# Lead and first block of an attention and two-layer MLP kernel emitted from one list, with five raw buffers, selected diagonals and sums per head pair

## Chip, cores and metric

One core of a Trainium2 chip runs the whole program. The metric is the device time of one execution in microseconds. The kernel before takes 912.47 us (median of three runs, 911.75 to 913.42).

## What is computed

A linear attention with decay over 4 batches, 8 heads, 768 steps and head size 48, then two MLP layers over the 3072 tokens of width 384 with hidden width 2048:

```python
for t in range(S):
    cur = np.einsum('bhd,bhe->bhde', u[None] * kt, vt)
    y[:, :, t] = np.einsum('bhd,bhde->bhe', rt, state + cur)
    state = w[None, :, :, None] * state + np.einsum('bhd,bhe->bhde', kt, vt)
x = y as (3072, 384)
r = np.maximum(x @ w_in, 0.0);  x = (r * r) @ w_out
h = x @ moe2_w_in;              out = (h - np.tanh(h)) @ moe2_w_out
```

## The kernel before

**Tiles.** The sequence is cut into 24 chunks of 128 steps, numbered 0 to 23: 0 to 3 are the first chunks of the four batches, 4 to 7 the second, and so on. Four chunks are one block of 512 tokens, so there are six blocks. Each MLP layer has 16 units of 128 hidden features. One unit of one block is a first product `gemm1` (tile `h`, nine matmuls of 512 columns), an activation, and a second product `gemm2` (three tiles `acc`, nine matmuls). Matmuls keep precision by parts: a weight is split in a high and a low part, so is the activation (`ghi`, `glo`), and three of the four products are summed.

**Weights** come as 64-bit numbers in raw tiles (`load_w`) and are converted by `conv0` (ScalarE, ACT), `conv1` (two instructions of VectorE, DVE), `conv2` (ACT, the high part) and `conv3` (DVE, the low part `w`). Layer 1's 16 weight tiles are converted while block 0 runs, one unit after the other. Layer 1 has four raw buffers; layer 2 takes two more from another pool.

**Lead.** The first four chunks need no state. `lead_a` multiplies r by k (`pr`) and applies the decays; `lead_p` forms the sums of u r k per step and head by matmul (tile `pk`, one matmul of 128 columns of weights per head pair) and transposes k; `lead_pa` copies both out on ACT and writes the diagonals of the score tile `am`; `lead_b` makes scores, `lead_m` masks them, `lead_c` makes the output y and the state, `lead_e` splits y into the tile `xt` that `gemm1` reads.

**Chunks from 4 on.** `load` fetches a chunk, `att_a` applies the decays (DVE), `att_k` the decay of the keys in natural order (GpSimd, POOL), `att_b` the scores `sc`, `att_v` the state update `pv`, `att_m` masks the scores into `ra`, whose diagonal holds u r k; `att_c` makes `y`, `att_e` splits it, `pack` moves 16 rows a head by six DMAs into place in `xt`. For chunks 4 to 7 the diagonal's sums come from matmuls (`att_diag`: 16 matmuls with one column, one per half chunk, head pair and head), are copied out by ACT, and are spread on the diagonal by one product with an identity on POOL (`att_d`) and eight activations on ACT (`att_da`). From chunk 8 on POOL and a DVE reduction make the sums, and POOL writes both halves of the diagonal.

**Order.** Instructions are issued per engine in the order in which the program emits them, and so are the DMAs of the queue SP. The lead is written out as a loop over four chunks at lines 870 to 915; block 0 is a loop over units in which `STEPS0` sets the units at which chunks 4 to 7 take their steps, and `gemm2`'s `glo` products are put off by one unit (`low_of`). Two lists are kept ahead: `front` issues `gemm1` and the activation two units early, `nat_q` holds POOL's work. Blocks 1 to 4 follow a fixed table (`visit`).

Of the kernel before, what the change touches and what calls it, by code (L numbers as in the profile page):

```python
# [25 lines left out]
def decay_attention_moe_moe_kernel(  # L26
# [10 lines left out]
    nc = tc.nc  # L37
# [11 lines left out]
    STEPS0 = ((1, 2, 3), (4, 5, 6), (8, 9, 10), (12, 13, 14))  # L49
    FILL = (0, 0, 4, 4)  # L50
# [179 lines left out]
    table = []  # L230

    def table_c():
        nc.vector.tensor_tensor(w96, pw[:, 0, :, 64:65], pw[:, 0, :, 32:33], op=ALU.mult)
        kh = gp.tile([GP, NP, L], F32, tag="g", name="kh")
# [3 lines left out]
        table.append(kh)  # L238

    def table_d():  # L240
        kh = table.pop()
        pt = bank(2, "pt")
        for p in range(NP):
            for a in range(2):
                q = slice(64 * a, 64 * a + D)
                nc.tensor.matmul(
                    pt[half(a), p * D:(p + 1) * D], lhsT=kh[q, p, :], rhs=ident[q, q], start=True, stop=True,
                )
        nc.scalar.activation(out=kt_tab, in_=pt[:, 0:GPS], func=AF.Copy)
# [39 lines left out]
    def att_s(i):  # L289
        bt_t[i] = a2.tile([128, 2, NP], F32, tag="bt", name="bt")  # L290
        nc.vector.tensor_reduce(
            out=bt_t[i].rearrange("p c P -> p (c P)"), in_=rn_t[i].rearrange("p (x d) -> p x d", d=D),
            axis=mybir.AxisListType.X, op=ALU.add,
        )
# [3 lines left out]

    def att_d(i, a):
        q = half(a)  # L300
        nc.gpsimd.tensor_tensor(
            ra_t[i][q, a],
            ident[q, q][:, None, None, :].to_broadcast([64, NP, 2, L]),
            bt_t[i][q].rearrange("p c (P o) -> p P c o", o=1).to_broadcast([64, NP, 2, L]),
            op=ALU.mult,
        )

    def att_da(i, a):
        q = half(a)
        for c in range(2):  # L310
            for p in range(NP):
                nc.scalar.activation(
                    out=ra_t[i][q, a, p, c, :], in_=ident[q, q], func=AF.Copy, scale=bt_t[i][q, c, p:p + 1]
                )

    def att_a(i):
        def sub(t):
            return t.rearrange("p P (c t) -> p P c t", c=2)

        def tab(t, n):  # L320
            return t[:, :, None, :].to_broadcast([n, NP, 2, L])

        r, k = rk_t[i][:, 0], rk_t[i][:, 1]
        if i < 2 * TPB:
            pr_t[i] = a2.tile([GP, NP, C], F32, tag="pr", name="pr")
            nc.vector.tensor_tensor(pr_t[i], r, k, op=ALU.mult)
            nc.vector.tensor_tensor(sub(r), sub(r), tab(tr[:, :, 32:96], GP), op=ALU.mult)
            for a in range(2):
                q = slice(64 * a, 64 * a + D)
                nc.sync.dma_start(out=ra_t[i][q, a].rearrange("p P c t -> p (P c t)"), in_=r[q].rearrange("p P t -> p (P t)"))  # L330
        else:
            for a in range(2):
                q = slice(64 * a, 64 * a + D)
                nc.vector.tensor_tensor(ra_t[i][q, a], sub(r[q]), tab(tr[q][:, :, 32:96], D), op=ALU.mult)
        nc.vector.tensor_tensor(sub(k), sub(k), tab(tr[:, :, 95:31:-1], GP), op=ALU.mult)
# [3 lines left out]
    def nat_push(i):  # L339
        if i < NTAU:  # L340
            G = nc.gpsimd
            if i < 2 * TPB:
                nat_q.append(lambda: att_k(i, G))
                return
# [27 lines left out]
    def att_diag(i, pb):  # L372
        bt = pb[:, 2 * GPS:2 * GPS + 2 * NP].rearrange("p (c P) -> p c P", c=2)
        for c in range(2):
            for p in range(NP):
                for a in range(2):
                    q = slice(64 * a, 64 * a + D)
                    nc.tensor.matmul(
                        bt[half(a), c, p:p + 1], lhsT=pr_t[i][q, p, c * L:(c + 1) * L],
                        rhs=ucol[q, p, a:a + 1], start=True, stop=True,  # L380
                    )
        bt_t[i] = a2.tile([128, 2, NP], F32, tag="bt", name="bt")
        nc.scalar.activation(out=bt_t[i], in_=bt, func=AF.Copy)
        att_d(i, 0)
        att_da(i, 1)

    def att_v(i):
        pb = pbank(i, 1, "pv")
# [10 lines left out]
        if i < 2 * TPB:  # L399
            att_diag(i, pb)  # L400
# [54 lines left out]
    def att_e(i):  # L455
# [24 lines left out]
    def lead_a(i):  # L480
        V = nc.vector
        r, k = rk_t[i][:, 0], rk_t[i][:, 1]
        V.tensor_tensor(pr_t[i], r, k, op=ALU.mult)
        if i:
            V.tensor_tensor(k, k, tk, op=ALU.mult)
            V.tensor_tensor(r, r, tr, op=ALU.mult)
            return
        up, down = pw[:, 0, :, 0:64], pw[:, 1, :, 64:0:-1]
        V.tensor_tensor(k[:, :, 0:64], k[:, :, 0:64], pw[:, 0, :, 63::-1], op=ALU.mult)
        V.tensor_tensor(k[:, :, 64:C], k[:, :, 64:C], pw[:, 1, :, 1:65], op=ALU.mult)  # L490
        V.tensor_tensor(r[:, :, 0:64], r[:, :, 0:64], down, op=ALU.mult)
        V.tensor_tensor(r[:, :, 64:C], r[:, :, 64:C], up, op=ALU.mult)
# [4 lines left out]
    def lead_p(i):  # L497
        pk = bank(1, "pk")
# [5 lines left out]
        for p in range(NP):  # L504
            nc.tensor.transpose(pk[:, p * GP:(p + 1) * GP], rk_t[i][:, 1, p, :], ident[0:GP, 0:GP])
        pk_t[i] = pk

    def lead_pa(i):
        pk = pk_t.pop(i)
        diag[i] = a2.tile([128, H], F32, tag="bt", name="bt0")  # L510
        nc.scalar.activation(out=diag[i], in_=pk[:, NP * GP:NP * GP + H], func=AF.Copy)
        nc.scalar.activation(
            out=kv_t[i][0], in_=pk[:, 0:NP * GP].rearrange("p (P x) -> p P x", x=GP), func=AF.Copy
        )
# [571 lines left out]
```

## Time and profile before

| | |
|---|---|
| median of three runs | 912.47 us |
| the profiled execution | 910.81 us |
| its span in the trace | 909.1 us |
| PE busy | 888.6 us, 98% |
| ACT busy | 640.3 us, 70% |
| DVE busy | 621.5 us, 68% |
| POOL busy | 219.5 us, 24% |
| mean granted clock of TensorE | 0.997 |
| one raw weight tile, by SP | 768 KB |
| one chunk: `rkt`, `kn`, two `vs` | 448, 192, 2 x 96 KB |
| one copy of `ra` | 96 KB, two a chunk |

Engines are called PE (TensorE, matmuls; PEld is its weight load), DVE, ACT, POOL, and SP for the DMA queue. An idle time in brackets is the time for which the engine waited just before the row, and behind the arrow stands what ended it. A matmul of full-precision numbers runs as two passes, so the trace shows twice as many as the program's rows.

### The profile page before, as it was taken

To read this page: it belongs to the slowest core of one execution; us is meant where nothing else is said; L and a number is where in the kernel's file an instruction comes from. 1 tells how busy PE (TensorE), PEld (TensorE's weight loads), DVE (VectorE), ACT (ScalarE), POOL (GpSimd) and SP (SyncE) were. 2 spreads that over 40 slices of the span, in tenths; PEclk is the share of its full clock that TensorE was granted. 3 is DMA by queue.
4 is the path that set the end of the run, shared out by engine and by line. 5 is a ranking of instruction groups with operands and counts; after the bars stand their busy time and mean duration, and the time that the engine had idled before them with its cause. 6 is when DMAs were issued, how large, how long until landed. Compare 5 with 4: busy or idle time off the path is not lost.

```text
span 909.1 us, 15201 instructions
## 1 busy us (share of the span) xinstructions
PE 888.6 (98%) x5852; PEld 732.2 (81%) x5852; DVE 621.5 (68%) x1003; ACT 640.3 (70%) x1163; POOL 219.5 (24%) x204
## 2 busy tenths in 40 slices
PE   9799999999999999999999999999999999999997
PEld 7677788888888888888888777888888888888885
DVE  7788942531432252221377899999999999999996
ACT  5777754455444544454688888988988988988985
POOL 5211424554464456353101021001001010010000
PEclk9999999999999999999999999999999999999999
DMA  9766321312222131200763200200200200200000
GB/s 257 204 196 201 113 87 51 100 54 67 71 69 69 52 102 52 83 9 8 271 218 137 70 1 0 70 1 1 70 0 1 70 1 1 69 1 1 35 0 36
DMA packets 31177, 65.98 MB, mean 73 GB/s; under 512 B 5264, under 2 KB 16912, under 8 KB 31104
## 3 DMA queue, kind: packets, MB, share of 16 engines
q1 hardware_dynamic: 30976, 64.78, 22.9%
q8 instruction: 46, 0.75, 0.3%
q14 instruction: 27, 0.22, 0.1%
q10 hardware_dynamic: 128, 0.23, 0.1%
HBM read 52.79 MB, written 9.44 MB: 68 GB/s over the span
## 4 chain that ended last, share of the span: by engine, by line
PE 85%; DMA 4%; DVE 4%; ACT 4%; issue 2%; SPq 1%; POOL 0%; DVEq 0%; POOLq 0%; ACTq 0%
PE h L628 39%; PE o L786 20%; PE acc L676 20%; DMA raw<-in_w_dram 2%; PE sc L367 2%; PE y L447 2%; PE pv L394 2%; DMA first_v<-in_nat_dram 1%; DMA ra<-rkt 1%; DVE hy L732 1%; ACT raw L85 0%; SPq L474 0%; DVE raw L94 0%; ACT th L733 0%; DVE hy L751 0%
## 5 line engine op out<-in xcount | busy, mean ns | idle before, releaser
L628 PE MATMUL h<-xt,w 128*128 128x512 f32 x864 | 212.4, 390 | 1.6 <-ACT w L102 0.9
L628 PE MATMUL h<-xs,w 128*128 128x512 f32 x864 | 211.4, 389 | 0.0
L628 PEld LDWEIGHTS h<-xt,w 128*128 128x128 f32 x864 | 162.5, 188 | 36.4 <-ACT w L102 1.3
L628 PEld LDWEIGHTS h<-xs,w 128*128 128x128 f32 x864 | 162.2, 188 | 34.0
L642 ACT ACTIVATE g<-h 128x512 f32<-128x512 f32 x96 | 57.2, 596 | 150.4 <-PE h L628 150.3
L676 PE MATMUL acc<-ghi,w 128*128 128x512 f32 x576 | 152.8, 397 | 6.1 <-ACT ghi L645 6.1
L786 PE MATMUL o<-ghi,w 128*128 128x512 f32 x576 | 148.8, 390 | 0.3 <-ACT ghi L757 0.3
L676 PEld LDWEIGHTS acc<-ghi,w 128*128 128x128 f32 x576 | 106.6, 189 | 29.9 <-ACT ghi L645 7.5
L786 PEld LDWEIGHTS o<-ghi,w 128*128 128x128 f32 x576 | 107.6, 188 | 24.0 <-ACT ob L797 1.3
L466 DVE TENSOR_TENSOR ys<-y,ys 112x128 fp32r<-112x128 f32 x20 | 5.8, 292 | 172.0 <-ACT xt L464 172.0
L648 POOL TENSOR_TENSOR glo<-g,ghi 128x512 fp32r<-128x512 f32 x64 | 82.1, 1283 | 169.2 <-PE acc L676 98.6
L709 POOL TENSOR_TENSOR xs<-x2f,xs 128x512 fp32r<-128x512 f32 x18 | 24.4, 1355 | 313.5 <-DVE xs L708 313.5
L733 ACT ACTIVATE th<-h 128x512 f32<-128x512 f32 x96 | 57.5, 599 | 41.9 <-DVE hy L732 41.9
L786 PE MATMUL o<-glo,w 128*128 128x512 f32 x288 | 84.2, 394 | 2.0 <-DVE glo L763 1.9
L676 PE MATMUL acc<-glo,w 128*128 128x512 f32 x288 | 83.2, 390 | 0.9 <-DVE glo L657 0.9
L746 DVE SCALAR_TENSOR_TENSOR hy<-q,hy 128x512 f32<-128x512 f32 x96 | 78.2, 815 | 0.1
L732 DVE SCALAR_TENSOR_TENSOR hy<-h,y 128x512 f32<-128x512 f32 x96 | 66.0, 687 | 13.4 <-ACT y L730 13.3
L751 DVE COPY_PREDICATED hy<-mask,th 128x512 f32<-128x512 uint8 x96 | 70.8, 737 | 0.0
L736 DVE TENSOR_TENSOR th<-h,th 128x512 f32<-128x512 f32 x96 | 66.2, 689 | 5.9 <-ACT th L733 0.7
L734 ACT ACTIVATE q<-y,ba 128x512 f32<-128x512 f32 x96 | 68.7, 715 | 0.0
L737 ACT ACTIVATE q<-y,bb 128x512 f32<-128x512 f32 x96 | 68.5, 713 | 0.0
L740 ACT ACTIVATE mask<-y,bm 128x512 uint8<-128x512 f32 x96 | 68.3, 711 | 0.0
(113 smaller groups left out, 1191.7 us busy)
## 6 DMA issues: line engine op xcount, KB each, us to landing
raw<-in_w_dram SPq DMA_DIRECT2D x32, 768.0 KB, 5.1
rkt<-in_rk_dram SPq DMA_DIRECT2D x20, 448.0 KB, 4.1
x2d<-x2s SPq DMA_DIRECT2D x18, 256.0 KB, 2.3
x2f<-x2d SPq DMA_DIRECT2D x18, 256.0 KB, 3.5
out_dram<-ob SPq DMA_DIRECT2D x18, 256.0 KB, 2.2
kn<-in_nat_dram SPq DMA_DIRECT2D x20, 192.0 KB, 4.8
vs<-in_nat_dram SPq DMA_DIRECT2D x40, 96.0 KB, 4.2
rnt<-in_nat_dram SPq DMA_DIRECT2D x16, 192.0 KB, 4.5
```

Of the source, the lines that this page charges most:

```text
L628: nc.tensor.matmul(h, lhsT=w_in(layer, f, part, kk), rhs=x[:, xpart, kk, :], start=(n == 0), stop=(n == 3 * KK - 1),)
L648: nc.gpsimd.tensor_tensor(lo, g, hi.bitcast(F32), op=ALU.subtract)
L676: nc.tensor.matmul(acc[j][m], lhsT=w_out(1, e, part, m * 128, (m + 1) * 128), rhs=g, start=(f == 0 and n < KK), stop=(last and g is lo),)
L732: nc.vector.scalar_tensor_tensor(out=hy, in0=h, scalar=PK, in1=y, op0=ALU.mult, op1=ALU.mult)
L733: nc.scalar.activation(out=th, in_=h, func=AF.Tanh)
L734: nc.scalar.activation(out=q1, in_=y, func=AF.Square, bias=p2["ba"], scale=1.0)
L736: nc.vector.tensor_tensor(th, h, th, op=ALU.subtract)
L737: nc.scalar.activation(out=q2, in_=y, func=AF.Square, bias=p2["bb"], scale=1.0)
L740: nc.scalar.activation(out=mask, in_=y, func=AF.Sign, bias=p2["bm"], scale=1.0)
L746: nc.vector.scalar_tensor_tensor(out=hy, in0=q2, scalar=PD, in1=hy, op0=ALU.add, op1=ALU.mult)
L751: nc.vector.copy_predicated(hy, mask, th)
L786: nc.tensor.matmul(acc[j][m], lhsT=w_out(2, f, part, m * 128, (m + 1) * 128), rhs=g, start=(f == 0 and n == 0), stop=(f == NF - 1 and n == 2),
```

## The change

Seven things are changed.

- Lead and block 0 are one list, `first_order`, of 419 pieces such as `h.3` (the `gemm1` of unit 3) or `c1a.5` (the first instruction of `conv1` of weight tile 5). A function per name emits the piece; the steps of the old functions are split so that each can stand by itself. The list also holds the DMAs. It covers block 0, the first two `gemm1` of block 1 and the first steps of chunks 8 and 9. `STEPS0`, `low_of` and the loop of the lead are gone.
- Five raw buffers in one pool serve both layers.
- The diagonal of `ra` is written by an affine selection on POOL that reads the sums with a broadcast and keeps them where row and column agree; for all chunks from 4 on, both halves. `att_da` on ACT is gone.
- The sums of chunks 0 to 7 are made per head pair: eight matmuls with 112 x 64 weights and two columns in place of 16 matmuls with one column (chunks 4 to 7), or of four with 112 x 128 weights (chunks 0 to 3). ACT copies them out by four small activations for chunks 4 to 7.
- The decay of the keys in natural order runs on DVE for chunks 4 to 7.
- `rn` and `pr` share one tile; `att_s` writes its eight sums in another order.
- The second head quartet's diagonals in the lead are indexed by a general formula, with the same result.

```diff
     def load_w(layer, f):
-        pool, n = (cv, 4) if layer == 1 or f % 5 < 3 else (p2["pool"], 2)
-        raw = pool.tile([128, 2 * DM, 2], U32, tag="raw", name="raw", bufs=n)
+        raw = cv.tile([128, 2 * DM, 2], U32, tag="raw", name="raw", bufs=5)
...
+    def diagonal(out, values):
+        m, n, t = out.shape
+        nc.gpsimd.affine_select(
+            out=out, in_=values[:, :, None].to_broadcast([m, n, t]), compare_op=ALU.is_equal, fill=0.0, base=0,
+            pattern=[[0, n], [1, t]], channel_multiplier=-1,
+        )
+
     def att_d(i, a):
         q = half(a)
-        nc.gpsimd.tensor_tensor(
-            ra_t[i][q, a],
-            ident[q, q][:, None, None, :].to_broadcast([64, NP, 2, L]),
-            bt_t[i][q].rearrange("p c (P o) -> p P c o", o=1).to_broadcast([64, NP, 2, L]),
-            op=ALU.mult,
-        )
-
-    def att_da(i, a):
...
+        diagonal(ra_t[i][q, a].rearrange("p P c t -> p (P c) t"), bt_t[i][q])
...
-    def att_diag(i, pb):
-        bt = pb[:, 2 * GPS:2 * GPS + 2 * NP].rearrange("p (c P) -> p c P", c=2)
-        for c in range(2):
-            for p in range(NP):
-                for a in range(2):
-                    q = slice(64 * a, 64 * a + D)
-                    nc.tensor.matmul(
-                        bt[half(a), c, p:p + 1], lhsT=pr_t[i][q, p, c * L:(c + 1) * L],
-                        rhs=ucol[q, p, a:a + 1], start=True, stop=True,
-                    )
...
+    def att_sums(i):
+        bt = sum_t[i] = pb_t[i][:, 2 * GPS:2 * GPS + 2 * NP].rearrange("p (P a) -> p P a", a=2)
+        for p in range(NP):
+            for c in range(2):
+                nc.tensor.matmul(
+                    bt[64 * c:64 * c + 64, p, :], lhsT=pr_t[i][:, p, c * L:(c + 1) * L], rhs=ucol[:, p, :],
+                    start=True, stop=True,
+                )
...
+        for a in range(2):
+            for c in range(2):
+                nc.scalar.activation(out=bt_t[i][half(a), c::2], in_=bt[64 * c:64 * c + 64, :, a], func=AF.Copy)
...
+    def lead_sums(i):
+        pk = pk_t[i] = bank(1, "pk")
         for p in range(NP):
-            nc.tensor.matmul(
-                pk[:, NP * GP + 2 * p:NP * GP + 2 * p + 2], lhsT=pr_t[i][:, p, :], rhs=ucol[:, p, :],
-                start=True, stop=True,
-            )
+            for c in range(2):
+                nc.tensor.matmul(
+                    pk[64 * c:64 * c + 64, NP * GP + 2 * p:NP * GP + 2 * p + 2],
+                    lhsT=pr_t[i][:, p, c * L:(c + 1) * L], rhs=ucol[:, p, :], start=True, stop=True,
+                )
...
+    first_order = """
+        pr.0 pb.0 rk.2 rk.1 tk.0 v.1 k.0 r.0 tp.0 pr.2 pr.1 v.0 rk.3 L.4 kn.0 lb.0 lb.1 k.1 lbt.0 dg.0 pb.1
...
+        "nk": lambda i: att_k(i, V if i < 2 * TPB else G),
...
+        for item in first_order.split():
+            what, which = item.split(".")
+            make[what](int(which))
+        del acc[0]
+
+        nf = NF + 2
         for n, (layer, j, f) in enumerate(units):
+            if n < NF:
+                continue
```

How the order moves shows at three places. The first is PE at the attention of chunk 5. Before, its scores (`sc`), state update (`pv`) and sums (`pv` from `wu` and `pr`) stand together ahead of the `gemm2` of unit 2:

```order
L628 MATMUL h<-xt,w_3_662 128x512 x9
L367 MATMUL sc<-ra_103,rkt 64x64 x16
L394 MATMUL pv<-vs_99,kn_101 64x48 x16
L378 MATMUL pv<-wu,pr 64x1 x16
L676 MATMUL acc_671<-ghi,w_2_629 128x512
```

Now they are three visits with other products between them:

```order
L382 MATMUL sc<-ra_103,rkt 64x64 x16
L739 MATMUL acc_664<-glo,w_0_557 128x512
L739 MATMUL acc_665<-glo,w_0_557 128x512
L739 MATMUL acc_666<-glo,w_0_557 128x512
L414 MATMUL pv<-vs_99,kn_101 64x48 x16
L691 MATMUL h<-xt,w_4_727 128x512 x9
L393 MATMUL pv<-wu,pr 64x2 x8
L691 MATMUL h<-xt,w_5_740 128x512 x9
```

The low products of unit 0 and the `gemm1` of units 4 and 5 have moved in between, and the sums are half as many matmuls. The second place is DVE around the first converted weight tiles (the `raw` rows are the two instructions of `conv1`, the `w` rows are `conv3`, the rows to `xt` the low parts of the lead's y). Before:

```order
L108 TENSOR_TENSOR w_0_448<-raw,w_0_448 128x768
L419 TENSOR_TENSOR dec<-st,pw 112x192
L610 TENSOR_TENSOR xt<-y,xt 128x3x128
L93 TENSOR_SCALAR raw<-raw 128x768
L94 SCALAR_TENSOR_TENSOR raw<-raw 128x768
L108 TENSOR_TENSOR w_1_587<-raw,w_1_587 128x768
L433 TENSOR_TENSOR s_590<-dec,pv 112x192
```

Now:

```order
L112 TENSOR_TENSOR w_1_479<-raw,w_1_479 128x768
L89 TENSOR_SCALAR raw<-raw 128x768
L669 TENSOR_TENSOR xt<-y,xt 128x3x128
L93 SCALAR_TENSOR_TENSOR raw<-raw 128x768
L669 TENSOR_TENSOR xt<-y,xt 128x3x128
L112 TENSOR_TENSOR w_0_557<-raw,w_0_557 128x768
L89 TENSOR_SCALAR raw<-raw 128x768
L93 SCALAR_TENSOR_TENSOR raw<-raw 128x768
L112 TENSOR_TENSOR w_3_594<-raw,w_3_594 128x768
L456 TENSOR_TENSOR s_613<-dec,pv 112x192
```

Tile 1 is converted first, its instructions are mixed with others, and tile 3 is ready before the state step of chunk 4 (`s`), where only tiles 0 and 1 were. The third place is SP around the copy of the decayed r of chunk 4 (`ra`), which waits for DVE. Before:

```order
L71 DMA raw<-in_w_dram 128x1536 x2
L200 DMA rkt<-in_rk_dram 112x1024
L203 DMA kn_101<-in_nat_dram 128x384
L206 DMA vs_99<-in_nat_dram 64x384 x2
L860 DMA ub<-in_u_dram 64x192 x2
L330 DMA ra_102<-rkt 48x512 x2
L71 DMA raw<-in_w_dram 128x1536
```

Now:

```order
L68 DMA raw<-in_w_dram 128x1536
L342 DMA ra_102<-rkt 48x512 x2
L185 DMA first_v<-in_nat_dram 128x384
L68 DMA raw<-in_w_dram 128x1536 x3
L206 DMA rkt<-in_rk_dram 112x1024
L209 DMA kn_101<-in_nat_dram 128x384
```

The copy has moved ahead of the loads of chunk 5 and of one raw tile, and three raw tiles and the values of chunk 3 stand behind it.

## Rows read from the trace of the kernel before

**Rows 1.** The page, busy us, share of the span and instructions of an engine.

```profile
PE 888.6 (98%) x5852; PEld 732.2 (81%) x5852; DVE 621.5 (68%) x1003; ACT 640.3 (70%) x1163; POOL 219.5 (24%) x204
```

**Rows 2.** By stretch: busy PE, PEld, DVE, ACT, POOL; granted clock, DMA share, GB/s.

```profile
7.28:32.44 25.16, 23.38 (x416) 21.82 (x416) 20.87 (x41) 15.68 (x50) 8.00 (x9) 1.00 0.97 264
32.44:132.56 100.12, 90.46 (x789) 72.75 (x787) 78.21 (x115) 74.75 (x148) 25.82 (x19) 0.98 0.50 153
132.56:197.80 65.24, 65.24 (x615) 54.57 (x614) 25.16 (x47) 30.54 (x61) 33.52 (x30) 1.00 0.28 83
42.00:44.00 2.00, 2.00 (x6) 1.52 (x6) 1.90 (x5) 1.96 (x5) 0.00 (x0) 0.50 0.13 35
```

**Rows 3.** The waits of PE: who waited for whom, us, times, longest.

```profile
PE acc L676 <- ACT ghi L645: 6.1, 4, 2.4
```

**Rows 4.** Timeline of PE around the first `gemm1`: start, us, what, idle before it.

```profile
29.25 1.39 PE L367 MATMUL sc<-ra,rkt 48*64 48x64 f32 x31 [0.76 <-DMA ra<-rkt]
...
35.67 2.34 PE L628 MATMUL h<-xt,w 128*128 128x512 f32 x9 [0.88 <-ACT w L102]
40.41 1.90 PE L676 MATMUL acc<-ghi,w 128*128 128x512 f32 x4 [2.41 <-ACT ghi L645]
```

**Rows 5.** Timeline of PE behind block 0's last accumulation: one unit without attention.

```profile
132.56 2.20 PE L628 MATMUL h<-xt,w 128*128 128x512 f32 x9
...
136.64 2.20 PE L628 MATMUL h<-xt,w 128*128 128x512 f32 x9
```

**Rows 6.** Timeline of PE from chunk 4's `y` to chunk 5's attention.

```profile
46.66 1.15 PE L447 MATMUL y<-ra,vs 128*64 128x64 f32 x32
47.74 1.66 PE L676 MATMUL acc<-ghi,w 128*128 128x512 f32 x6
...
49.92 2.20 PE L628 MATMUL h<-xt,w 128*128 128x512 f32 x9
52.05 1.15 PE L367 MATMUL sc<-ra,rkt 48*64 48x64 f32 x32
...
53.96 1.06 PE L378 MATMUL pv<-wu,pr 48*64 48x1 f32 x32
54.95 1.65 PE L676 MATMUL acc<-ghi,w 128*128 128x512 f32 x6
```

**Rows 7.** Timeline of PE in the lead: the sums of chunk 0.

```profile
7.88 1.05 PE L500 MATMUL pk<-wu,first 112*128 112x2 f32 x8
8.79 0.58 PE L505 MATMUL pk<-ident,first 112*128 112x112 f32 x4
```

**Rows 8.** Timeline of DVE in block 0: low part of an activation, then one conversion.

```profile
45.63 0.69 DVE L657 TENSOR_TENSOR glo<-g,ghi 128x512 fp32r<-128x512 f32 x1
46.23 0.56 DVE L93 TENSOR_SCALAR raw<-raw 128x768 uint32<-128x768 uint32 x1
46.89 0.96 DVE L94 SCALAR_TENSOR_TENSOR raw<-raw 128x768 uint32<-128x768 uint32 x1
47.78 0.94 DVE L108 TENSOR_TENSOR w<-raw,w 128x768 fp32r<-128x768 f32 x1
```

**Rows 9.** Timeline of the queue SP around chunk 4's copy of `ra`.

```profile
22.27 4.08 SPq L330 DMA_DIRECT2D ra<-rkt  x2
27.46 0.35 SPq L71 DMA_DIRECT2D raw<-in_w_dram  x1
```

**Rows 10.** Forms on POOL up to 400 us: busy us, mean ns, idle before.

```profile
L301 POOL TENSOR_TENSOR ra<-ident,bt 64x512 f32<-64x512 f32 x34 | 36.8, 1084 | 48.4 <-ACT bt L383 27.5 <-PE pv L378 11.7 <-issue 6.9
...
L266 POOL TENSOR_SCALAR_AFFINE_SELECT ident<-ident 128x128 f32<-128x128 f32 x1 | 0.3, 292 | 0.1
```

**Rows 11.** Timeline of all engines near 84 us: POOL and DVE.

```profile
84.18 1.01 POOL L275 TENSOR_TENSOR rnt<-rnt,ub 128x384 f32<-128x384 f32 x1 [8.16 <-DMA vs<-in_nat_dram]
84.24 1.50 DVE L657 TENSOR_TENSOR glo<-g,ghi 128x512 fp32r<-128x512 f32 x1
```

**Rows 12.** Timeline of DVE at 35 us: its longest idle time in block 0.

```profile
35.65 0.96 DVE L108 TENSOR_TENSOR w<-raw,w 128x768 fp32r<-128x768 f32 x1 [4.98 <-ACT w L102]
```

More of the change, by code (lines that the diff above doesn't have):

```diff
@@ L337, in decay_attention_moe_moe_kernel, with att_rd, att_k0 @@
+    def att_rd(i):
+        for a in range(2):
+            q = slice(64 * a, 64 * a + D)
+            nc.sync.dma_start(
+                out=ra_t[i][q, a].rearrange("p P c t -> p (P c t)"),
+                in_=rk_t[i][q, 0].rearrange("p P t -> p (P t)"),
+            )
+    def att_k0(i):
+        k = by_half(rk_t[i][:, 1])
+        nc.vector.tensor_tensor(k, k, tr[:, :, None, 95:31:-1].to_broadcast([GP, NP, 2, L]), op=ALU.mult)
+    def att_a(i):
+        att_r0(i)
+        att_k0(i)
     nat_q = []
@@ L508, in lead_pa @@
[L508 to L513, printed above, removed]
-        )
-        for h in range(4, H):
-            z, a = divmod(h - 4, 2)
-            nc.scalar.activation(
-                out=am_b[(2 * i + 1) % 4][:, 2 * a + z], in_=ident, func=AF.Copy, scale=diag[i][:, h:h + 1]
-            )
@@ new lines, in lead_turn, with lead_bt, lead_kn @@
+    def lead_turn(i):
+        for p in range(NP):
+            nc.tensor.transpose(pk_t[i][:, p * GP:(p + 1) * GP], rk_t[i][:, 1, p, :], ident[0:GP, 0:GP])
+    def lead_bt(i):
+        diag[i] = a2.tile([128, H], F32, tag="bt", name="bt0")
+        nc.scalar.activation(out=diag[i], in_=pk_t[i][:, NP * GP:NP * GP + H], func=AF.Copy)
+    def lead_kn(i):
+        nc.scalar.activation(
+            out=kv_t[i][0], in_=pk_t[i][:, 0:NP * GP].rearrange("p (P x) -> p P x", x=GP), func=AF.Copy
+        )
@@ L591, in lead_c, with lead_cs @@
                     )
+        lead_y[i] = yv
+    lead_pv = {}
+    def lead_cs(i):
+        kn, vn = kv_t[i]
         pt = bank(2, "pt")
@@ L657, in act1_low, with gemm2_terms @@
             nc.vector.tensor_tensor(lo, glow.pop((j, f)), hi.bitcast(F32), op=ALU.subtract)
[L659 to L679 removed]
+    def gemm2_terms(j, f, terms):
+        if f == 0 and j not in acc:
+            acc[j] = [bank(m, f"acc{m}") for m in range(KK)]
+        hi, lo = gq[1, j, f]
+        for n, m in terms:
+            part, g = ((0, hi), (1, hi), (0, lo))[n]
+            nc.tensor.matmul(
+                acc[j][m], lhsT=w_out(1, f, part, m * 128, (m + 1) * 128), rhs=g,
+                start=(f == 0 and n == 0), stop=(f == NF - 1 and n == 2),
+            )
@@ new lines, in gemm2_1, with evac1_part @@
+    def gemm2_1(j, f):
+        terms = [(n, m) for n in range(3) for m in range(KK)]
+        if f == NF - 1:
+            terms.sort(key=lambda t: t[1])
+        gemm2_terms(j, f, terms)
+    def evac1_part(j, m):
+        if m == 2 and j == NB - 1:
+            t = gp.tile([128, TB], F32, tag="g", name="x2s")
+        elif m == 2 and j == NB - 2:
+            t = p2["pool"].tile([128, TB], F32, tag="q2", name="x2s")
+        else:
+            t = stg.tile([128, TB], F32, tag="x2s", name="x2s", bufs=3)
+        if m % 2 and j < NB - 1:
+            nc.vector.tensor_copy(t, acc[j][m])
+        else:
+            nc.scalar.activation(out=t, in_=acc[j][m], func=AF.Copy)
+        nc.sync.dma_start(out=x2d[j][:, m, :], in_=t)
@@ L693, in evac1 @@
-            nc.sync.dma_start(out=x2d[j][:, m, :], in_=t)
+            evac1_part(j, m)
         del acc[j]
@@ L842, in decay_attention_moe_moe_kernel @@
         first(0)
-        first(1)
         setup_pool()
```

440 lines of the change are left out of this document (192 added, 248 removed).

## The prediction

> **What bounds the kernel now.** I read four views in turn. The page first: TensorE (PE) is busy 888.6 of 909.1 us [rows 1], so about 20 us of idle time is all that an order can win, unless work itself goes away. Then busy time by stage: from 7.28 us (the warm-up matmuls are over) to 32.44 us (first matmul of `gemm1`) PE is busy 23.38 of 25.16 us; from there to 132.56 us (last accumulation of block 0) 90.46 of 100.12; in the 65 us behind that it never stops [rows 2]. I call the first stretch the lead and the second block 0. Nothing that the change moves lies behind them but the diagonals on POOL, so the forecast is made in these 125.3 us; I take it that what is won there stays won, since PE is without a gap when it leaves them.
>
> Third, the waits: PE's largest is 6.1 us, `acc` for `ghi` of ACT [rows 3]. Fourth, the timeline: the gaps open at single pieces, 0.76 us for `ra` by DMA, 0.88 for `w`, 2.41 for `ghi` [rows 4]. In block 0 the timeline has nine of them, which come to 9.6 us. ACT and DVE are busy 75 and 78 of 100 us there [rows 2], so it is not lack of engine time: ACT and DVE work in order, and a piece needed soon stands behind one that waits. Behind the gaps at 35 to 40 us the granted clock is 0.50, the lower of its two levels, 1.2 GHz [rows 2].
>
> **What block 0 costs now.** One `gemm1` and one `gemm2` take 4.08 us (132.56 to 136.64), so 18 of the one and 16 of the other are 18 x 2.04 + 16 x 2.04 = 69.4 us [rows 5]. A chunk's `y` takes 1.08 us, `sc` with `pv` 1.91, the 32 passes of the sums 0.99 [rows 6]. With `y` four times (chunks 4 to 7), `sc` and `pv` four times (5 to 8) and the sums three times (5 to 7) that is 69.4 + 4.3 + 7.6 + 3.0 = 84.3 us of work. The stretch is 100.1, so 15.8 are lost: 9.6 idle; 1.8 for some 3.6 us at half clock (40.41 to 44 us); 1.8 for eight changes to attention and back, since a `gemm1` before attention is 2.13 long instead of 2.04 and the `gemm2` behind it 2.18, 0.23 together [rows 6]; and the remaining 2.6 for pipelines that run empty at the gaps.
>
> **The change, part by part.**
>
> *Sums per head pair.* 32 passes with 48 x 64 weights and one column become 16 passes with 112 x 64 weights and two columns. The nearest row is `y`: weights of 128 or 112 x 64, 32 passes in 1.08 us, 0.034 each, so 0.54 instead of 0.99 [rows 6]. In the lead 8 passes with 112 x 128 weights (0.91 us) become 16 of the same new form, 0.54 too; from the other side they cannot cost more than the lead's old pass, 0.114, which makes 1.82 us for a set [rows 7]. I take 0.54, as the weights have that shape: 3 x 0.45 = 1.4 us less in block 0. The four sets of the lead (0.37 each) lie before the first `gemm1`, where DVE decides (below), and count nothing. At the other end the three sets of block 0 cost 3 x 1.28 = 3.8 us more than I take, and the five before the first `gemm1` put off PE there by 6.4.
>
> *The finer order.* Attention on PE comes in 12 separate visits instead of 8, at 0.23 us each [rows 6]: +4 x 0.23 = 0.9 us. The Trainium skill, TensorEngine Tiling, section Tiling Modes, speaks against cutting attention finer: a change of tiling mode drains the engine, and these rows agree with 0.23 us a visit. Also one `lead_cs` (16 passes at the same 0.034, 0.55 us) now stands behind the first `gemm1`: +0.55.
>
> *The first `gemm1`.* DVE is busy 20.87 us in the lead [rows 2]. Before the first `gemm1` the new order wants of it the same work and the conversion of one weight tile further, 0.66 + 0.89 [rows 8], and the k decay of chunk 4, which no row prices on DVE: above 0, below the 0.60 from one 512-column piece to the next [rows 8]; I take 0.5 for 384 columns, which makes 2 us for chunks 4 to 7. So DVE, never idle, is ready at 7.3 + 20.9 + 2.0 = 30.2; PE's own work would allow 28.2 (32.44 less 1.8 idle, 4 x 0.37 and 0.45 for sums, and 0.55), or 34.6 with the sums at their dear end. I add 1.5 us for gaps on DVE, which was idle for 4.3 us of the lead: first `gemm1` at 31.7 instead of 32.4, -0.7. The transfers: in the lead the DMA engines are at 0.97 with 264 GB/s [rows 2]; up to weight tile 2 the new list asks for 6.8 MB, there soon after 26 us at that rate. The `ra` copy of chunk 4 holds SP's queue until `ar.4` is done; it was issued at 22.27 and the next weights at 27.46 [rows 9]. DVE has some 12.5 us of pieces ahead of the end of `ar.4`, from 6.1 us on, an estimate from rows like [rows 8], so it ends near 19, and the weights behind it go out some 5 us earlier, though three stand behind it now.
>
> *Block 0.* 69.4 + 4.3 + 7.6 + 3 x 0.54 + 0.55 = 83.5 us, and 12 x 0.23 = 2.8 for visits. The waits that stay I put at 3 us: adding up the pieces in the new order by the rows' durations (an estimate), DVE has converted the weights 1.3 to 1.6 us before PE wants them in the first 25 us of the block, and over 4 us after that; one held piece eats the small margin. At the end the six packing DMAs of chunk 7 leave SP about as PE comes to `h.16`. Together 89.3 instead of 100.1: -10.8. The cold clock goes with the 2.41 us gap.
>
> *Diagonals on POOL.* For chunks 4 to 7 eight selections replace four products on POOL and 32 activations on ACT. A 64 x 512 product takes 1.08 us; a 128 x 128 selection 0.29 [rows 10], which scaled by columns is 1.16. I take 1.1: POOL does as much as before, since four k decays leave it, and it has the time (33.5 of 65 us in the next block [rows 2]). Bounds: 0.29, and no row excludes far more (rival 4).
>
> *Five raw buffers and the rest.* One more weight can be on its way; in layer 2 five were in flight already, from two pools: nothing. The strided sum of `att_s`: nothing, DVE is under half busy in the middle blocks [rows 2].
>
> **Sum.** -0.7 - 10.8 = -11.5 us. The profiled execution took 910.8 us, so 899.3; it lies 1.7 below the median 912.5 of the runs shown, and against that I forecast **901 us**.
>
> **The rivals.**
>
> 1. *Every wait closes.* First `gemm1` at 30.2 and 0.5 us of waits: -2.2 - 13.3 = -15.5, or 897. For it: the order fits the rows' durations. Against it: in-order engines do not run as rows add up. 0.08.
>
> 2. *DVE becomes the bound.* Its work in the 125.3 us is 99.1 us [rows 2], with the k decay 101; the forecast stretch of 113.8 wants it 0.89 busy. In block 0 it reached 0.78. If it gets to 0.85 the stretch is 119 us, -6.4: **906 us**. For it: DVE is slowed by POOL. A difference of 128 x 512 that takes 0.69 us [rows 8] took 1.50 where POOL began a product 0.06 us earlier [rows 11]. The Trainium skill, SBUF — State Buffer, section SBUF: two separate sides, has it that the two share a port pair as an exclusive lock, held for the whole instruction; that trace agrees. By this rule a selection on POOL holds DVE as the product did, and nothing is won by the change of operation. Against it: the old gaps of DVE had other causes, 4.98 us at once for ACT's `w` [rows 12], which stood behind eight diagonal activations that are gone. 0.20.
>
> 3. *The waits only move.* Each wait that closes makes the next piece late, and the time stays within 0.2%. For it: PE's gaps have different releasers, DMA, ACT and DVE [rows 3, 4]. Against it: 1.8 us of clock and over 1 us of sums go in any case. 0.05.
>
> 4. *The selection is dear.* With a broadcast input it is in no row. The next block has 65.2 us, of which POOL is busy 33.5, 8.7 of them (8 x 1.08) in diagonals; 40.4 us are free for eight selections. From 5.05 us each POOL sets the pace of the four middle blocks. At 6 us a block gets 7.6 us longer, 30 in all: 931 us. It decides against the change from 5.4 us on, where four blocks lose 11.5. For it: POOL's cost for a new form is unknown. Against it: the 0.29 us row would have to be 18 times short. 0.06.
>
> **How the numbers follow.** The forecast has 0.61; 898 to 904 is its own range, by 0.5 to 6 us of waits. About 0.2% is what a measurement of this kernel can tell from no change, here 1.8 us. Forecast and rivals 1 and 2 are all faster: 0.89. Same 0.05, slower 0.06. The range runs from 897 (rival 1, just within) to 908, which takes in rival 2 and the dear end of the sums: +3.8 in block 0 and +2.9 for a first `gemm1` at 34.6.
>
> **What would show it.** Right: first `gemm1` near 31 to 32 us, the last accumulation of block 0 near 121, PE's `acc` for `ghi` wait under 2 us, clock 1.00 from 8 us on, the 16 passes of sums about 0.54 us, selections near 1.1 us, and PE without a gap behind block 0. Wrong: gaps of PE whose releaser is a DVE `w` or `glo` piece (rival 2), selections over 5 us (rival 4), `raw` waits behind the `ra` copies on SP, or a gap at the first matmul of block 1 behind the packing DMAs. If the gaps of block 0 close and the total does not fall, it would be wrong that the gain stays won.

## The result, and the profile after

The changed kernel takes 899.93 us (median of four runs, 899.52 to 901.51) against 912.58 for the kernel before: a ratio of 0.9865, 95% interval 0.9848 to 0.9882. The forecast was 901 us. The execution shown here took 899.92 us, its span is 898.2. Of all executions reported below one, of e5, ran in a slow state (1553.64 us at a mean granted clock of 0.688) and is left out of its figures.

The page's line of busy times, to be held against [rows 1]: PE is busy 1.7 us less in a span that is 10.9 us shorter.

```profile
PE 886.9 (99%) x5820; PEld 730.0 (81%) x5820; DVE 616.5 (69%) x1007; ACT 632.6 (70%) x1143; POOL 200.7 (22%) x204
```

Busy time by stage (columns as in [rows 2]): lead, block 0, the 65 us behind it.

```profile
6.31:33.44 27.13, 25.04 (x416) 22.11 (x417) 22.36 (x48) 16.17 (x48) 4.28 (x10) 0.87 0.83 255
33.44:120.97 87.53, 87.53 (x758) 70.78 (x755) 68.67 (x110) 65.04 (x130) 17.62 (x14) 1.00 0.58 174
120.97:186.20 65.23, 64.98 (x612) 54.02 (x611) 28.33 (x51) 31.16 (x63) 35.96 (x36) 1.00 0.28 83
```

Block 0 runs without one pause of PE, at clock 1.00, and is 12.6 us shorter than the 100.12 of [rows 2]. The lead is where the time came back: its mean clock is 0.87, and the first `gemm1` starts at 33.44, 1.0 us later than before. Behind block 0 the span has 898.2 - 120.97 = 777.2 us left, before 909.1 - 132.56 = 776.5, so what block 0 won stays won but for 0.7.

All waits of PE, whole span. The 6.1 us of [rows 3] are gone; 1.4 us for `first` (the lead's r and k) are new.

```profile
PE o L858 <- DVE glo L835: 1.9, 3, 1.0
PE warm L264 <- POOL low L271: 1.6, 1, 1.6
PE pk L546 <- DVE first L521: 1.4, 1, 1.4
PE acc L739 <- DVE glo L731: 0.9, 1, 0.9
PE pk L553 <- POOL vz L621: 0.4, 1, 0.4
PE o L858 <- ACT ghi L829: 0.3, 1, 0.3
PE pk L553 <- ACT bt L557: 0.3, 1, 0.3
PE acc L739 <- DVE x2s L758: 0.3, 1, 0.3
```

The new wait in the timelines of DVE and PE, and the granted clock behind it by stage:

```profile
9.66 0.69 DVE L521 TENSOR_TENSOR first<-first 112x512 f32<-112x512 f32 x1 [1.13 <-DMA first<-in_rk_dram]
...
10.50 0.63 PE L546 MATMUL pk<-wu,first 112*64 112x2 f32 x16 [1.35 <-DVE first L521]
```

```profile
11.00:12.00 1.00, 0.73 (x9) 0.65 (x6) 1.00 (x4) 0.18 (x1) 0.10 (x1) 0.74 0.98 225
12.00:18.00 6.00, 6.00 (x66) 5.36 (x67) 4.35 (x10) 2.10 (x7) 1.31 (x4) 0.50 1.05 302
18.00:19.00 1.00, 1.00 (x16) 0.81 (x14) 0.00 (x0) 0.17 (x1) 0.00 (x0) 0.84 0.98 399
```

The r k product of chunk 1 waits for its DMA until 9.66, because the new list loads chunk 2 (`rk.2`) ahead of chunk 1 (`rk.1`); PE stands for 1.35 us. Between 11 and 12 us the clock falls to its lower level, and between 18 and 19 us it is back.

The parts of the work, from the timelines of DVE and PE, and from the groups by form (busy us, mean ns):

```profile
24.99 0.55 DVE L293 TENSOR_TENSOR kn<-kn,kt_tab 128x384 f32<-128x384 f32 x1
25.46 0.56 DVE L89 TENSOR_SCALAR raw<-raw 128x768 uint32<-128x768 uint32 x1
...
32.88 0.63 PE L393 MATMUL pv<-wu,pr 112*64 112x2 f32 x16
33.44 2.33 PE L691 MATMUL h<-xt,w 128*128 128x512 f32 x9
```

```profile
L311 POOL TENSOR_SCALAR_AFFINE_SELECT ra<-bt 64x512 f32<-64x512 f32 x40 | 32.0, 801 | 56.9 <-ACT bt L403 54.4
```

A set of sums takes 33.44 - 32.88 = 0.56 us, a k decay 25.46 - 24.99 = 0.47. A selection takes 0.80 in the mean of the first 400 us; the eight in block 0 are dearer (below).

### The profile page after: what moved, and what is told of

Its sections match the earlier page's. It is cut to its first block, busy times and chain, and to the rows that moved or that the text cites. A ratio compares the mean times of both kernels' runs of the same rounds, so it can differ in the third digit from the quotient of the medians.

```text
span 898.2 us, 15122 instructions
## 1 busy us (share of the span) xinstructions
PE 886.9 (99%) x5820; PEld 730.0 (81%) x5820; DVE 616.5 (69%) x1007; ACT 632.6 (70%) x1143; POOL 200.7 (22%) x204
## 4 chain that ended last, share of the span: by engine, by line
PE 94%; DVE 2%; ACT 2%; DMA 1%; issue 0%; POOL 0%; SPq 0%; DVEq 0%
PE h L691 42%; PE acc L739 22%; PE o L858 20%; PE sc L382 2%; PE y L479 2%; PE pv L414 2%; DMA first<-in_rk_dram 1%; DVE hy L804 1%; PE sc L591 0%; PE y L631 0%; ACT th L805 0%; DVE hy L823 0%; PE y L636 0%; ACT y L802 0%; DVE th L808 0%
## 5 line engine op out<-in xcount | busy, mean ns | idle before, releaser
L739 PE MATMUL acc<-ghi,w 128*128 128x512 f32 x576 | 150.5, 394 | 0.3 <-DVE x2s L758 0.3
```

Source lines behind the costliest of these rows:

```text
L739: nc.tensor.matmul(acc[j][m], lhsT=w_out(1, f, part, m * 128, (m + 1) * 128), rhs=g, start=(f == 0 and n == 0), stop=(f == NF - 1 and n == 2),
```

## The experiments

Two questions were open: why the lead is late, and whether block 0's gain is the order's or that of the parts moved off ACT and PE. The kernel before took 911.51, 913.17 and 913.82 us (medians) beside the three sets of runs below; where sets are compared, the ratios to it are used.

### The lead

**Chunk 1 loaded first (e1_rk1_first).**

```diff
-        pr.0 pb.0 rk.2 rk.1 ... tp.0 pr.2 pr.1 v.0
+        pr.0 pb.0 rk.1 rk.2 ... tp.0 pr.1 pr.2 v.0
```

> The list with chunk 1's r and k loaded ahead of chunk 2's, and its product made first; nothing else. Theory (the lead's new loss is the load of chunk 1 that lands at 9.6 us, the 1.35 us gap of PE behind it, and the lower clock from 11 to 18 us that follows, about 3.5 us): no gap at 9 to 10.5 us, granted clock 1.00 through the lead, first gemm1 at 30 to 31.5 us instead of 33.4, block 0 still 87.5 us long, 896.5 to 898. Rival (DVE decides when the first gemm1 can start, as the prediction had it, at 31.7): first gemm1 at 32 or later, 898.5 to 899.5. Rival (the clock falls for some other reason than this gap): clock 0.50 in the same place, 899 to 900.

Measured: 899.9 us (899.29 to 900.07), ratio 0.9869 (0.9852 to 0.9886), nothing gained. PE's timeline has the pause one step later:

```profile
11.73 0.98 PE L553 MATMUL pk<-ident,first 112*128 112x112 f32 x4 [1.17 <-ACT bt L557]
```

The key piece of chunk 1 (`k.1`) stands on DVE behind the product of chunk 2 (`pr.2`), which now has the late DMA. The first `gemm1` is at 33.54. The time is that of the last rival, but as the pause has only moved, the run cannot tell whether the clock falls for another reason.

**Ten warm-up matmuls in the pause (e3_fill).** They stand ahead of chunk 1's sums.

```diff
-        ... k.1 lbt.0 dg.0 pb.1
+        ... k.1 lbt.0 dg.0 fi.10 pb.1
```

> Ten more warm-up matmuls on PE just ahead of the sums of chunk 1, where it waits for 1.35 us; the loads as in the change. Theory (the lower clock costs more than the wait): clock 1.00 from 11 to 18 us, the wait as long as before or filled, first gemm1 at 30.5 to 32 us, 897 to 898.5. Rival (the wait costs, the clock is harmless because DVE or a load ends last anyway): first gemm1 at 33 to 34, 899.5 to 900.5.

Measured: 898.77 us (896.87 to 900.29), ratio 0.9856 (0.9833 to 0.9879). They take 1.27 us, PE pauses only 0.28 us, the clock stays at 1.00 until 14 us and is 0.50 until 17.5; the first `gemm1` is at 32.46. In the execution shown the fall came later and was shorter. The time lies between the two sides, and its interval takes in the change's 0.9865, so a gain is not shown.

**Chunk 1 first, its k piece too (e2_rk1_k1).**

```diff
-        pr.0 pb.0 rk.2 rk.1 ... tp.0 pr.2 pr.1 ... lb.1 k.1 lbt.0
+        pr.0 pb.0 rk.1 rk.2 ... tp.0 pr.1 ... lb.1 k.1 pr.2 lbt.0
```

> The list with chunk 1's r and k loaded before chunk 2's, and with DVE's key piece of chunk 1 (k.1) ahead of the r k product of chunk 2 (pr.2), which stands later. Theory (the 1.7 us that the first gemm1 is late come from PE gaps of 1 us and more in the lead, behind which the clock falls; loading chunk 1 first alone moved the gap from the sums to the transposes, as k.1 stood behind pr.2): no gap of PE over 0.5 us between 9 and 13 us, granted clock 1.00 from 9 to 20 us, first gemm1 at 30.5 to 32 us, 897 to 898.5 us. Rival (the clock falls there whatever the gap, or another gap takes its place): a stretch at 0.50 between 9 and 20 us stays, first gemm1 above 33 us, 899.5 to 900.5 us.

Measured: 897.21 us (896.59 to 898.95), ratio 0.9825 (0.9803 to 0.9847). The pauses at 9 to 12 us are down to 0.4 us, yet in the profiled execution the clock fell all the same (0.50 from 12 to 18 us), with the first `gemm1` at 32.45. The other executions tell more: mean clocks 0.995, 1.000, 0.997, 1.000, 0.997 with spans of 897.2, 894.9, 895.8, 895.2, 895.5. So neither side of the expectation holds as it was put, though the time is in the theory's range: the same program runs with a long fall and with a short one or none, and the long one costs about 2 us.

**The change once more (e11_after_again)**, unchanged, for its executions:

> The changed kernel once more, beside the others on one chip: how its executions differ among themselves. Theory (its 1.35 us pause at 9 us makes the clock fall in nearly every execution): mean granted clock 0.996 or less in at least four of the executions, 899 to 901.5 us. Rival (whether the clock falls is chance and the pause has no part in it): at least two executions at 0.998 or more, and those 2 us faster than the others.

Measured: 899.1 us (897.62 to 900.46), ratio 0.9844 (0.9819 to 0.9869). Two executions at 0.995 (900.46 and 899.73 us), two at 0.998 (897.62 and 898.46): 2.1 us apart in the mean. The theory's four in four was wrong, and what the rival asked for came. Counted over all runs of lists that keep the pause (the change, e1, e11, and e10 below), 3 of 17 executions had 0.998 or more; without it (e2, e9) 6 of 9. The pause therefore seems to make the fall likelier, but not certain. The mean clock is a coarse sign of it: the execution of e3 that was shown has 0.998 with 3.5 us at 0.50. With the line drawn at 0.997 it is 3 of 17 against 8 of 9.

**Both, and two short fills (e9_rk1_k1_fill).**

```diff
-        pr.0 pb.0 rk.2 rk.1 ... r.0 tp.0 pr.2 pr.1 ... k.1 lbt.0 ... r.1 tp.1
+        pr.0 pb.0 rk.1 rk.2 ... r.0 fi.4 tp.0 pr.1 ... k.1 pr.2 lbt.0 ... r.1 fi.4 tp.1
```

> The list with chunk 1 first (r and k of chunk 1 loaded ahead of chunk 2's, k.1 ahead of pr.2) and four 256-column matmuls of the warm-up ahead of the transposes of chunk 0 and four ahead of those of chunk 1, some 0.5 us each by the 0.127 us of one in the run with ten. Theory (the clock of the lead falls in some executions and not in others of the same program, the more seldom the fewer pauses PE makes at 9 to 12 us; a fall costs 2 us or a little more): mean granted clock 0.997 or more in every execution, times of 896 to 897.5 us, median 896.5. Rival (the fall does not depend on what PE does there): one execution in two still at 0.996 or less, times spread from 896.5 to 899.5 us, median 897.5 or above. Second rival (PE has no time to spare in the lead): every time 1 us longer than without the eight matmuls.

Measured: **896.32 us** (895.81 to 897.39), ratio 0.9815 (0.9792 to 0.9839), mean clock 0.998 to 1.000 in all four executions. It is the fastest version; beside it on one chip the change took 899.1, and its slowest execution (897.39) is under the fastest of the change (897.62). Lead and block 0 by stage, and the timelines of DVE and PE at the first `gemm1`:

```profile
6.17:29.33 23.16, 22.95 (x426) 20.06 (x425) 22.13 (x48) 16.12 (x47) 3.98 (x11) 1.00 0.94 297
29.33:116.86 87.53, 87.53 (x758) 70.80 (x755) 68.79 (x110) 65.09 (x130) 17.95 (x14) 1.00 0.58 174
```

```profile
28.45 0.56 DVE L669 TENSOR_TENSOR xt<-y,xt 128x384 fp32r<-128x384 f32 x1
...
29.33 2.33 PE L691 MATMUL h<-xt,w 128*128 128x512 f32 x9
```

Block 0 has the same 87.53 us to the hundredth; all of the 4.1 us by which this span (894.1) is shorter lie in the lead. PE is busy 22.95 of 23.16 us there: at full clock the lead is PE's own work, so the eight fills may themselves cost up to the 1.0 us that they take. DVE's last piece for the first `gemm1` ends at 29.01, 0.3 us before it. That the fills keep the clock up is not shown: e2 without them has 0.997 or more in four of five executions.

### Order or parts

**All the parts, the old order (e7_parts_only).** The loop of the lead, `STEPS0` and `low_of` are back; sums per pair, selections, k decay on DVE and five buffers stay.

```diff
-        for item in first_order.split():
-            what, which = item.split(".")
-            make[what](int(which))
+    STEPS0 = ((1, 2, 3), (4, 5, 6), (8, 9, 10), (12, 13, 14))
...
+        att_k(4, nc.vector)
```

> The kernel before with all the parts of the change but the list: five raw buffers, selections on POOL, sums per head pair, k decay of chunks 4 to 7 on DVE, in the old order. Theory (the order closes PE's waits; the parts give the sums' 1.4 us and take eight activations a chunk out of ACT's way): block 0 95 to 99 us instead of 100.1, gaps of 6 us or more left, 907 to 910.5. Rival (the waits of block 0 came from the diagonals on ACT and from the fourth buffer, so the parts close them without the list): block 0 under 92 us, 900 to 904.

Measured: 915.34 us (913.44 to 916.44), ratio 1.004 (1.0025 to 1.0054): **slower than before**, and outside both sides. Block 0 takes 99.75 us (36.43 to 136.18), hardly less than before; the loss is in the lead, whose first `gemm1` is 4.0 us later. The waits of DVE and PE:

```profile
DVE kn L283 <- DMA kn<-in_nat_dram: 5.0, 1, 5.0
...
PE acc L671 <- ACT ghi L640: 7.9, 4, 2.9
PE sc L533 <- DVE am L544: 3.7, 1, 3.7
PE h L623 <- DVE w L107: 2.2, 1, 2.2
```

In the old order the k decay of chunk 4 stands ahead of the lead's work, and DVE waits 5.0 us there for keys that SP brings late. On POOL this piece had waited too (14.2 us for three of them before), and PE for none of that.

**The same with the k decay on POOL (e8_parts_k_pool).**

```diff
-        att_k(4, nc.vector)
+        att_k(4, nc.gpsimd)
```

> All the parts of the change on the old order (lead as a loop, block 0 by units), but the k decay of chunks 4 to 7 left on POOL, where it cannot hold DVE ahead of the lead. Theory (the parts are worth their work, the order is worth the waits): sums of three chunks 1.3 us less, ACT without its 32 diagonal activations; block 0 keeps gaps of 6 us and more, its stretch is 95 to 99 us, 906 to 911 us in all. Rival (ACT's freed time closes the waits without the new order): the gaps of block 0 under 3 us, 900 to 904 us. Second rival (parts cost something in this order whatever engine decays k): 913 us or more.

Measured: 910.64 us (908.24 to 912.42), ratio 0.9969 (0.9955 to 0.9983). The parts alone are worth 2.8 us. The execution shown does not tell where: its block 0 is 0.7 us shorter than before, and its lead, in which the clock fell, 1.2 us longer. ACT's 32 activations are gone, and block 0 still waits:

```profile
PE acc L671 <- ACT ghi L640: 7.5, 4, 2.9
...
33.61:132.99 99.38, 89.41 (x743) 71.57 (x739) 79.51 (x115) 69.15 (x128) 22.91 (x23) 0.98 0.49 154
```

**The new order, old parts (e6_old_parts).** One-column sums, product and activations for the diagonals, k decay on POOL: the three diffs of e4, e5 and e10 below in one.

> The new order with the old parts: sums in one-column matmuls, diagonals by product on POOL and, for chunks 4 to 7, by eight activations on ACT for one half, k decay on POOL. Theory (the order alone closes the waits of block 0): the old sums cost 3.5 us as measured with the sums alone, the rest at most 2 us more, block 0 with gaps under 3 us in all: 903 to 906 us. Rival (the order needs the freed ACT): ACT's 32 activations return to block 0, gaps of 4 us and more for ghi or w, 908 us or more.

Measured: 907.89 us (904.18 to 909.0), ratio 0.9929 (0.9904 to 0.9955), between the two that were expected. Order alone 0.9929, parts alone 0.9969; multiplied 0.9898, while the change is at 0.9865 (0.9844 when repeated). Some 3 to 5 us come only when both are there, an estimate that the intervals leave uncertain by about 3 us. By stage, the lead of the execution shown is 4.2 us longer than with the change (first `gemm1` at 37.68, behind a pause of 2.54 us and a longer fall) and block 0 4.8 us (92.32). The next two take this apart.

**The new order with the old sums (e4_old_sums).**

```diff
-                bt[64 * c:64 * c + 64, p, :], lhsT=pr_t[i][:, p, c * L:(c + 1) * L], rhs=ucol[:, p, :],
+                bt[half(a), 2 * p + c:2 * p + c + 1], lhsT=pr_t[i][q, p, c * L:(c + 1) * L], rhs=ucol[q, p, a:a + 1],
```

> The change with the sums made as before: one column per head for chunks 4 to 7 and 128-column weights in the lead; order, selections, buffers and k decay as in the change. Theory (passes with 112 x 64 weights cost 0.034 us): each set of chunks 5 to 7 0.99 us instead of 0.56, block 0 longer by 1.3 us, the lead by 0 to 1.5, 901 to 902.7. Rival (a set costs what its weights cost, whatever the form): no difference, 899.9.

Measured: 903.45 us (901.33 to 904.79), ratio 0.9908 (0.989 to 0.9927). The total misses the theory's range by 0.8 us, and the rival is out. Block 0 has no wait and takes 89.02 us (36.73 to 125.75), 1.5 more than with the new sums, as expected. The lead is what was missed: the first `gemm1` is at 36.73 instead of 33.44, 3.3 us later and not 0 to 1.5. In this execution the clock was 0.50 from 12 to 20 us, and dear sums of the lead lie in that stretch. Those of chunks 1 and 2:

```profile
10.68 1.25 PE L545 MATMUL pk<-wu,first 112*128 112x2 f32 x8 [0.51 <-DVE first L521]
...
14.17 1.86 PE L545 MATMUL pk<-wu,first 112*128 112x2 f32 x8
```

**The new order with the old diagonals (e5_old_diag).**

```diff
-        diagonal(ra_t[i][q, a].rearrange("p P c t -> p (P c) t"), bt_t[i][q])
+        if i < 2 * TPB and a:
+            for c in range(2):
+                for p in range(NP):
+                    nc.scalar.activation(out=ra_t[i][q, a, p, c, :], in_=ident[q, q], ...
+            return
+        nc.gpsimd.tensor_tensor(ra_t[i][q, a], ident[q, q]..., bt_t[i][q]..., op=ALU.mult)
```

> The change with the old diagonals: a product with the identity on POOL (1.08 us against 0.80 for the selection), and for chunks 4 to 7 one half by eight activations on ACT. Theory (the selection only takes work off engines that have time): block 0 without a gap over 0.5 us or with gaps of 1 us in all, POOL busy 10 us more over the run, 899.5 to 901.5 us. Rival (ACT's eight activations a chunk were what held the pieces): gaps of PE for ghi or w in block 0, 904 us or more.

Measured: 903.36 us (902.25 to 904.49, five executions), ratio 0.989 (0.9868 to 0.9912): more than the theory's 901.5, just under the rival's 904, by the rival's mechanism with another last link. The timelines of ACT, DVE and PE give the chain, and the stages (block 0, then the time behind the gap) its price:

```profile
63.60 2.01 ACT L321 ACTIVATE ra<-ident,bt 64x64 f32<-64x64 f32 x8
...
65.65 0.73 DVE L437 COPY_PREDICATED ra<-low,sc 64x512 f32<-64x512 uint32 x1 [2.56 <-ACT ra L321]
...
75.01 0.63 PE L406 MATMUL pv<-wu,pr 112*64 112x2 f32 x16 [1.89 <-DVE s L469]
```

```profile
33.23:124.45 91.22, 89.33 (x758) 71.92 (x755) 69.80 (x110) 72.29 (x162) 15.69 (x10) 0.98 0.56 168
76.00:78.00 2.00, 2.00 (x26) 1.79 (x24) 1.87 (x4) 1.92 (x7) 1.43 (x1) 0.50 0.00 0
```

Eight activations of chunk 5 end 2.01 us after 63.60, DVE's masked copy waits 2.56 us for them, and DVE then works without a pause up to 75 us, so everything behind it is late, among it the state piece `s` for which PE stands 1.89 us; behind that the clock is 0.50. Block 0 is 3.7 us longer. e6 has the same wait of DVE, and PE stands 1.7 us. So the order is fitted so closely that 2 us more of ACT at one place break it. In the new order the old sums cost 0.9908 - 0.9865, some 4 us, and the old diagonals 0.9890 - 0.9865, some 2; together that is about what e6 loses against the change, where the old order gave 2.8 us for all parts. How the 3 to 5 us split between ACT's wait and the clock of the lead is not shown.

**The new order with the k decay on POOL (e10_nk_pool).**

```diff
-        "nk": lambda i: att_k(i, V if i < 2 * TPB else G),
+        "nk": lambda i: att_k(i, G),
```

> The change with the k decay of chunks 4 to 7 left on POOL in the new order. Theory (DVE has the time in the new order and POOL has it too, so the place of this piece counts nothing here): 899 to 900.5 us, block 0 without a gap over 0.5 us. Rival (POOL's product holds DVE and is itself late behind a selection, so pv or the scores wait): a gap of PE of 1 us or more at a pv of chunks 4 to 7, 902 us or more.

Measured: 900.27 us (899.24 to 901.58), ratio 0.9861 (0.9836 to 0.9885), no gap in block 0. Where this piece runs counts nothing that shows in the new order; in the old it decides between 1.004 and 0.9969, some 6 us.

## Why the prediction came out right, and what in it was wrong

That the total was only 1 us off is luck. The sum itself gave 899.3 against 899.92 for the execution shown, as two terms missed in opposite directions: block 0 by -1.8 us, the first `gemm1` by +1.7, with +0.7 behind block 0 that was put at nothing. The 1.7 us added because the profiled execution before lay below its median had no counterpart: that of the change lies at its median.

- **Block 0** was put at 89.3 us; it took 87.53. Of the 3 us of waits, none came: the 1.3 to 1.6 us by which the weights were to be ahead was enough. Work and visits were put at 86.3, so 1.2 came on top. There are 13 visits of attention, not 12 (0.23). The other 1.0 is `sc` and `pv`, put at 1.91 us a pair from a visit in which they stand together; in the new order they stand apart, as at chunk 5:

```profile
48.04 1.15 PE L382 MATMUL sc<-ra,rkt 48*64 48x64 f32 x32
49.12 0.97 PE L739 MATMUL acc<-glo,w 128*128 128x512 f32 x3
50.01 1.13 PE L414 MATMUL pv<-vs,kn 64*64 64x48 f32 x32
51.08 2.34 PE L691 MATMUL h<-xt,w 128*128 128x512 f32 x9
```

  From start to start `sc` takes 1.08 and `pv` 1.07, and over the four chunks 8.6 us where 7.6 was summed. The 69.4 us of `gemm1` and `gemm2`, the 4.3 of `y`, the 0.54 a set of sums (0.56), and that the cold stretch goes with the 2.41 us gap, held.
- **The first `gemm1`** failed: 31.7 was forecast, 33.44 came. The step said that DVE decides there, that sums in the lead count nothing, and that the clock is 1.00 from 8 us on. In the execution shown the clock fell for 7 us, and PE decided: 25.04 us busy, and DVE waited 3.0 us for `sc`. The sums count: with the old ones the first `gemm1` is 3.3 us later (e4, whose fall is also longer). The `ra` copy, forecast near 19 us, was issued at 22.62; in e9, without the fall, at 18.43. The order of the two loads, `rk.2` ahead of `rk.1`, stands in the diff's first line of the list; I followed SP's queue only around `ar.4`. Without pause and fall (e9) the first `gemm1` is at 29.33. PE's own limit of 28.2 comes out near, as e9 has eight fills of some 1.0 us besides, but by two misses: e9's lead starts at 6.17 us and not 7.28, and has 21.9 us of PE's own work where 20.9 was summed. DVE's 30.2 was 1.2 too late (29.0).
- **Behind block 0**: put at no change but for the diagonals, it lost 0.7 us, 0.25 of it a gap at 123.65 for DVE's copy `x2s`. The list reaches past block 0 and orders this copy too (its pieces `ev`).
- **Rival 2, DVE as bound**: it was busy 22.36 + 68.67 = 91.0 us of the stretch where 101 was forecast. 3.2 us of it lie in the next block (28.33 against 25.16 of [rows 2]), and DVE's forms got shorter, as the groups by form show: the first instruction of `conv1`, before, after, and in the old order with the new parts (e7),

```profile
L93 DVE TENSOR_SCALAR raw<-raw 128x768 uint32<-128x768 uint32 x16 | 10.5, 658 | 0.0
```

```profile
L89 DVE TENSOR_SCALAR raw<-raw 128x768 uint32<-128x768 uint32 x16 | 8.9, 554 | 0.0
```

```profile
L92 DVE TENSOR_SCALAR raw<-raw 128x768 uint32<-128x768 uint32 x16 | 11.0, 684 | 0.0
```

  POOL's busy time in block 0 does not explain it: 25.8 us before and 17.6 after, but 18.9 in e7, where the form is as long as before, and 21.9 in e10, where it is 584 ns. It goes with the order; which pieces no longer meet was not taken apart. The Trainium skill, SBUF — State Buffer, section SBUF: two separate sides, has DVE and POOL lock each other out for whole instructions. Here POOL had the worse of it, as its timeline and DVE's show:

```profile
88.96 4.50 POOL L311 TENSOR_SCALAR_AFFINE_SELECT ra<-bt 64x512 f32<-64x512 f32 x2 [12.50 <-ACT bt L403]
...
89.34 0.95 DVE L93 SCALAR_TENSOR_TENSOR raw<-raw 128x768 uint32<-128x768 uint32 x1
90.21 0.95 DVE L112 TENSOR_TENSOR w<-raw,w 128x768 fp32r<-128x768 f32 x1
```

  Two selections took 4.50 us, where the other three pairs of block 0 took 2.0 to 2.3 and those of the next blocks 1.3, while DVE's pieces beside them kept the 0.95 of [rows 8]. That fits the rule if DVE's pieces came first; the rows do not show who held what. PE waited for neither.
- **Rival 1, every wait closes**: true of block 0, and in e9, another list, of the lead but for 0.2 us; e9 took 896.3, near its 897. **Rival 3, waits only move**: true of block 0 in the old order with the new parts (e7, e8), not of the list. **Rival 4**: far off, though in block 0, where 1.1 us was taken, the eight selections took 10.9 us, 1.36 each; the mean of 0.80 comes from the blocks behind it.
- **Diagonals** were costed as "POOL does as much as before". Their worth is on ACT: with the old ones block 0 is 3.7 us longer (e5), though ACT has 22 us to spare there.

## What to carry to other kernels

An order fitted to the last microsecond and the parts that make room for it are one change: alone they gave 0.7% and 0.3%, together 1.4%, and the parts in the wrong order lost 0.4%, as a moved piece took a 5 us wait along to an engine with work queued behind it. Follow every load of the new order through its queue, the first ones too: one pair in the other order, with the piece behind it, was worth some 2 to 4 us here (e2, 0.9825 against 0.9844 and 0.9865). Price a piece from rows in which it stands as it will stand: `sc` and `pv` cost 0.24 us more a chunk apart than together. Where the granted clock differs among executions of one program, look at several before a fall is put down to a pause.

## What was unexpected of the hardware

The granted clock of the lead is not a matter of pauses alone. e7 and e8 have the same lead on PE up to 15 us, busy throughout from 8 us on; in one execution the clock stayed at 1.00, in the other it was halved. By stage, e7 and then e8:

```profile
8.00:11.00 3.00, 3.00 (x65) 2.67 (x61) 2.88 (x6) 1.83 (x7) 1.30 (x2) 1.00 1.07 252
11.00:12.00 1.00, 1.00 (x15) 0.84 (x14) 0.99 (x3) 0.58 (x3) 0.32 (x2) 1.00 1.02 248
```

```profile
8.00:11.00 3.00, 3.00 (x66) 2.67 (x64) 2.88 (x6) 1.70 (x6) 1.35 (x3) 1.00 1.05 252
11.00:12.00 1.00, 1.00 (x14) 0.75 (x10) 0.98 (x4) 0.40 (x2) 0.00 (x0) 0.66 1.06 296
12.00:17.00 5.00, 5.00 (x45) 4.71 (x46) 3.37 (x7) 1.77 (x6) 0.51 (x1) 0.50 1.05 307
```

The durations say the same as the clock: the scores of chunk 1, in e7 and then e8, in PE's timelines.

```profile
11.58 1.16 PE L533 MATMUL sc<-first 48*128 48x128 f32 x16
```

```profile
12.04 2.08 PE L533 MATMUL sc<-first 48*128 48x128 f32 x16
```

The Trainium skill, TensorE: Matmul & The Clock Gate, section Part 1, lets the clock fall after the engine has been idle. The trace differs: e8's rows show the fall with PE busy at every moment shown. What the runs support is a chance: in the new order, pauses of about 1 us and more at 9 to 12 us go with a mean clock under 0.998 in 14 of 17 executions, none or short ones in 3 of 9. What sets it in a single execution stays open.
